# First forward step and last inverse step as single full-precision products, and an earlier first tile table

## The chip, the cores and the metric

The kernel runs on one core of a Trainium2 chip. The metric is the time of one execution on the device in microseconds (us). The engines are TensorE (PE, with its weight loads shown as PEld), VectorE (DVE), ScalarE (ACT), GpSimd (POOL) and SyncE (SP), which issues most DMAs. TensorE's granted clock is shown as a share of 2.4 GHz: 1.00 is 2.4 GHz, 0.50 is 1.2 GHz.

## What is computed

A spectral layer is followed by a mixture of experts. `x` is 8 batches of 2496 tokens with 256 features.

```python
X = np.fft.rfft(x, axis=1)
Yr = Xr @ w_r - Xi @ w_i + b_r          # Yi likewise
Yr = sign(Yr) * maximum(abs(Yr) - 0.01, 0)
y = np.fft.irfft(Yr + 1j * Yi, n=2496, axis=1)
x = y.reshape(19968, 256)
expert = argmax(x @ w_gate, axis=1)     # 8 experts, gate_w is the softmax value
out[rows of e] = gate_w * (maximum(x[rows of e] @ w1[e], 0) @ w2[e])
```

## The kernel before

**Stages.** The transform of length 2496 is done as 39 times 64. `fwd_a` is the first forward step: 11 products `pa` per batch, with 117 (or 78) rows in and 120 out, 512 columns each, written to the scratch `spec` in memory. `turn` reads it back as `t`, `fwd_b` makes the second step (`pb`), `halves` splits the result into a rounded part and a rest (`sh`, `sl`), `mix` multiplies by the weights (`pk`, `pm`), with the sum `kb` of bias and `k` made on GpSimd, and `shrink` applies the threshold (`r`, then four operations `y`). `inv_b` (`pv`, evicted to `z`) and `inv_a` go back: `pz` turns a group of three times 39 tokens upright and computes the gate's logits in the same product, `py` is the last inverse step, evicted by ScalarE to `yb`. A batch has 22 groups. `route` (VectorE work, with one small product `pr` that counts tokens by expert) finds each token's place, and `scatter` sends the rows on GpSimd to a list per expert in memory. The experts then work on tiles of 256 rows.

**Full precision and splits.** PE takes full-precision numbers, or numbers of a rounded type at a higher rate. Most products here use the rounded type three times: rounded part by rounded part, rest by rounded part, rounded part by rest. `split_x` (L269) makes `xh` on ScalarE and `xl` on VectorE from `x`, one step of the schedule ahead of `fwd_a` (L280), which then makes three products `pa` for batches 1 to 7. For batch 0 it makes one full-precision product. In `inv_a` (L387) the bank `pz` is evicted twice, as `zh` by ScalarE and then `zl` by VectorE, and `py` is three products. `pz`, `pb` and `pv` are full-precision products.

**Order.** `spectral` (L411) runs 80 steps (batch b, s from 0 to 9), and PE, SP, ScalarE and VectorE execute in the order in which the code is written. A step begins with `fwd_b` and the first part of `halves` for the next step, `shrink` of the last, then `mix` of its own. The lists `first`, `second`, `loads` and `back` say which `fwd_a`, `split_x`, loads of `x` and `inv_b` fall into it. In the steps with s from 2 to 5 (`turning`) up to three calls of `inv_a` for the batch before are spread over the step by `inverse()`. `tick(n)` advances the oldest waiting `route` or `table` by n pieces (a piece ends at a `yield`), and `send(n)` issues n scatters. Both work through one queue, so more pieces in `route` put its later operations further back in the order.

**Banks and buffers.** `pa`, `pz` and `pv` share four PSUM buffers `u`; `py`, `pk`, `pr` share two, `yo`.

**Tables and the end.** `table(0)` (L638) tells which expert and rows the first five tiles take. It is queued in step s=6 of the last batch and counts all batches but one. `finish_last` (L531) does the last batch's `inv_a`, its `route` and `table(1)`, and runs tiles 0 to 2 between, with `tick` and `send` in them. `experts_rest` runs the others.

Of the kernel before, what the change touches and what calls it, by code (L numbers as in the profile page):

```python
# [10 lines left out]
F32 = mybir.dt.float32  # L11
# [8 lines left out]
S = 2496  # L20
# [78 lines left out]
class Kernel:  # L99
    def __init__(self, tc, nb, x, w_r, w_i, b_r, b_i, w_gate, w1, w2,  # L100
                 c_fa, c_fe, c_ga, c_bm, c_bi, c_ids, c_score, c_base, c_ltri, c_tcol, out):
        self.__dict__.update({n: v for n, v in locals().items() if n != "self"})
        self.nc = tc.nc
        self.ntok = nb * S
        self.cap = TT + self.ntok
        self.nt = (self.ntok + E * (TT - 1)) // TT
        done = (nb - 1) * S
        self.early = EARLY if done - E * (TT - 1) > (EARLY - 1) * TT else 0
        self.spec = [self.nc.dram_tensor(f"spec{i}_dram", (120, G, D), F32, kind="Internal").ap() for i in range(2)]
        self.xs = self.nc.dram_tensor("xs_dram", (E * self.cap, XW), F32, kind="Internal").ap()  # L110
# [31 lines left out]
    def open_inverse(self, st):  # L142
# [24 lines left out]
        self.gar = k.tile([120, 117], F32, name="gar")  # L167
        self.gh = k.tile([120, 117], F32R, name="gh")
        self.gl = k.tile([120, 117], F32R, name="gl")
        self.ids = k.tile([117, nb, G], I32, name="ids")  # L170
# [9 lines left out]
    def open_forward(self, st):  # L180
# [7 lines left out]
        self.far = far = f.tile([117, 120], F32, name="far")  # L188
        self.fh = f.tile([117, 120], F32R, name="fh")
        self.fl = f.tile([117, 120], F32R, name="fl")  # L190
        self.fer = f.tile([78, 120], F32, name="fer")
        self.feh = f.tile([78, 120], F32R, name="feh")
        self.fel = f.tile([78, 120], F32R, name="fel")
        nc.sync.dma_start(far, self.c_fa)
# [41 lines left out]
    def split_constants(self):  # L236
        nc, f, raw = self.nc, self.f, self.raw
        nc.scalar.copy(self.fh, self.far)
        nc.vector.tensor_sub(self.fl, self.far, self.fh)
        nc.scalar.copy(self.feh, self.fer)  # L240
        nc.vector.tensor_sub(self.fel, self.fer, self.feh)
        ws = self.w.tile([128, 2, D], F32, tag="r", name="wsum")
# [4 lines left out]
        for nm in ("s", "d", "r"):  # L247
# [3 lines left out]
            nc.vector.tensor_sub(self.wl[nm], raw[nm], self.wh[nm])  # L251
        nc.scalar.copy(self.gh, self.gar)
        nc.vector.tensor_sub(self.gl, self.gar, self.gh)
        for c in range(2):
# [13 lines left out]

    def split_x(self, b, q, g):  # L269
        nc = self.nc  # L270
        m = 117 if q < 5 else 78
        xt = self.xg[b, q][:m, g:g + 2, :].rearrange("p g d -> p (g d)")
        xh = self.w.tile([117, 512], F32R, tag="xh", name="xh")
        xl = self.w.tile([117, 512], F32R, tag="xl", name="xl")
        nc.scalar.copy(xh[:m, :], xt)  # L275
        nc.vector.tensor_sub(xl[:m, :], xt, xh[:m, :])  # L276
        self.xs2[b, q, g] = xh, xl

    def fwd_a(self, b, q, g):
        nc = self.nc  # L280
        m = 117 if q < 5 else 78
        raw, hi, lo = (self.far, self.fh, self.fl) if q < 5 else (self.fer, self.feh, self.fel)
        p = self.psi.tile([128, 512], F32, tag="u", name="pa", bufs=4)
        if b:
            xh, xl = self.xs2.pop((b, q, g))
            parts = ((hi, xh), (lo, xh), (hi, xl))
        else:
            parts = ((raw, self.xg[b, q][:, g:g + 2, :].rearrange("p g d -> p (g d)")),)
        for i, (a, v) in enumerate(parts):
            nc.tensor.matmul(p[:120, :], a[:m, :], v[:m, :], start=i == 0, stop=i == len(parts) - 1)  # L290
        ae = self.xp.tile([120, 2, D], F32, tag="ae", name="ae", bufs=5)
        to = ae.rearrange("p g d -> p (g d)")
# [94 lines left out]
    def inv_a(self, b, i):  # L387
        nc = self.nc
        for g in (2 * i, 2 * i + 1) if i < GH else ():
            p = self.psi.tile([128, 512], F32, tag="u", name="pz", bufs=4)  # L390
            for c in range(2):
                nc.tensor.matmul(p[:120, c * 136:(c + 1) * 136],
                                 self.z[:, c, 3 * g:3 * g + 3, :].rearrange("p j a -> p (j a)"), self.iw[:, c, :],
                                 start=True, stop=True)
            h = self.wi.tile([120, YW], F32R, tag="zh", name="zh", bufs=4)
            l = self.wi.tile([120, YW], F32R, tag="zl", name="zl", bufs=4)
            nc.scalar.copy(h, p[:120, :YW])
            nc.vector.tensor_sub(l, p[:120, :YW], h)
            self.hl[g] = h, l
        for g in (2 * i - 2, 2 * i - 1) if i else ():  # L400
            if g % GH == 0:
                self.yb = self.wi.tile([117, GH, YW], F32, tag="yb", name="yb", bufs=2)
            h, l = self.hl.pop(g)
            p = self.psi.tile([128, 512], F32, tag="yo", name="py")
            for m, (a, v) in enumerate(((self.gh, h), (self.gl, h), (self.gh, l))):
                nc.tensor.matmul(p[:117, :YW], a, v, start=m == 0, stop=m == 2)
            nc.scalar.copy(self.yb[:, g % GH, :], p[:117, :YW])
            if g % GH == GH - 1:
                self.jobs.append(self.route(b, g // GH, self.yb))

    def spectral(self, fwd):  # L411
        nb = self.nb
        self.t1s, self.pbs, self.ss, self.us, self.ys, self.hl, self.xs2 = {}, {}, {}, {}, {}, {}, {}
        self.jobs, self.rows = [], []
# [21 lines left out]

        first, second, loads, back = ({i: [] for i in range(-1, n)} for _ in range(4))
        for b in range(1, nb):
            at = 10 * b - 10
            for i, o in enumerate((1, 1, 2, 2, 3, 3, 4, 4, 5, 5, 6) if b == 1 else (-3, -2, -1, 0, 0, 1, 2, 3, 4, 5, 6)):  # L440
                first[at + o].append((b, *pairs[i]))
                second[at + o - 1].append((b, *pairs[i]))
            for q, o in enumerate((None, None, 0, 1, 1, 2) if b == 1 else (-7, -5, -4, -2, 0, 2)):
# [10 lines left out]
        for it in range(n):  # L454
            b, s = todo[it]
            late = b == nb - 1
            half, small = iter(()), iter(())
            if it + 1 < n:
                self.fwd_b(*todo[it + 1])
                half = self.halves(*todo[it + 1])  # L460
                next(half)
            if it:
                small = self.shrink(*todo[it - 1])
                next(small)
            next(half, None)
            turning = b and 2 <= s < 6
            turns = iter(range(3 * s - 6, 3 * s - 3) if turning else ())
# [7 lines left out]

            spare = 1 if late else 0
            self.tick(2 + spare)
            inverse()
            mix = self.mix(b, s)
# [6 lines left out]
            next(small, None)  # L486
            for a in second[it]:
                self.split_x(*a)
            self.tick(2 + spare)
# [11 lines left out]
            if it + 4 < n:  # L501
                self.turn(*todo[it + 4])
            if late and self.early and s == 6:
                self.jobs.append(self.table(0))
# [53 lines left out]
    def route(self, b, hf, y):  # L558
# [41 lines left out]
        nc.vector.tensor_copy(sb, pa[:, GH - 1, :])  # L600
        for _ in range(4):
            yield
# [35 lines left out]
    def table(self, last):  # L638
# [70 lines left out]
        if last:  # L709
            lap = rt.tile([128, 128], F32, name="lap")  # L710
            nc.vector.tensor_copy(lap, fin[:, 3:4].broadcast_to((128, 128)))
            yield "pe"
            p = self.psi.tile([128, 512], F32, tag="yo", name="pl")
# [255 lines left out]
```

## Time and profile before

| what | value |
|---|---|
| median of 3 runs | 1668.5 us (1666.49 to 1670.34) |
| the profiled execution's own time | 1668.7 us |
| its span, first to last instruction | 1666.9 us, mean granted clock 0.974 |
| PE busy | 1534.7 us (92%) |
| DVE busy | 1335.3 us (80%) |
| ACT busy | 1116.1 us (67%) |
| POOL busy | 617.5 us (37%) |

Busy time of PE counts overlapping matmuls once, and the ends of matmuls are modelled: the distance between the starts of two of them tells more of their cost than the length of one. A wait in brackets, such as `[3.94 <-DVE sb L600]`, is idle time of the engine ahead of the instruction and what ended it. In the table by stretch the number behind a busy time is a count of instructions.

### The profile page before, as it was taken

What the parts mean: (1) busy time and instruction counts of PE and PEld (TensorE: products, weight loads), DVE (VectorE), ACT (ScalarE), POOL (GpSimd) and SP (SyncE); (2) the same over time, 40 slices, a digit from 0 to 9 for tenths busy, and PEclk for the clock granted to TensorE, in tenths of its full rate; (3) what the DMA queues carried; (4) which work ended last, traced back from release to release, by engine and by line L of the source; (5) the groups of instructions that cost most, each with busy time, mean ns of one, the idle gap of its engine ahead of it and who ended that gap; (6) DMA issues with size and microseconds to landing.
All of it is one profiled execution on the core that took longest, in us unless ns stands there. A gap on an engine that the chain in (4) does not pass through costs nothing. (4 is left out here: it accounts for less than half of the span.)

```text
span 1666.9 us, 36023 instructions
## 1 busy us (share of the span) xinstructions
PE 1534.7 (92%) x10880; PEld 1422.8 (85%) x10880; DVE 1335.3 (80%) x2755; ACT 1116.1 (67%) x2334; POOL 617.5 (37%) x462
## 2 busy tenths in 40 slices
PE   5889898988988887779999999999999999999997
PEld 2778787878878886778999999999999999999996
DVE  2678878888888888668888888888888888888886
ACT  2677777676767665546677677677677667677675
POOL 2121626362535345351333333333333333333332
PEclk8899999999999998999999999999999999999998
DMA  8753535353535311324322312312312313213210
GB/s 249 200 145 94 171 98 161 108 156 107 164 95 148 102 57 46 114 65 102 97 50 46 99 47 46 100 46 60 85 46 61 83 46 96 49 46 91 52 46 19
DMA packets 182932, 153.81 MB, mean 92 GB/s; under 512 B 120378, under 2 KB 154080, under 8 KB 182477
## 3 DMA queue, kind: packets, MB, share of 16 engines
q1 hardware_dynamic: 162829, 107.17, 25.6%
q0 software_dynamic: 19904, 44.29, 8.1%
q8 instruction: 88, 1.44, 0.4%
q14 instruction: 111, 0.91, 0.2%
HBM read 243.33 MB, written 66.37 MB: 186 GB/s over the span
## 5 line engine op out<-in xcount | busy, mean ns | idle before, releaser
L892 POOL DMA_INDIRECT out<-o,row x154 | 303.7, 1972 | 571.2 <-DVE o L890 546.1
L882 PE MATMUL po<-h,hh 128*128 128x512 f32 x1312 | 463.4, 397 | 2.7 <-ACT hh L849 2.7
L844 PE MATMUL ph<-xh,l 128*128 128x256 f32 x1312 | 372.0, 284 | 4.4 <-DVE l L785 4.4
L844 PE MATMUL ph<-xh,h 128*128 128x256 f32 x1312 | 372.4, 284 | 0.6 <-ACT h L784 0.5
L844 PE MATMUL ph<-xl,h 128*128 128x256 f32 x1312 | 371.8, 283 | 0.2 <-DVE xl L827 0.2
L849 ACT ACTIVATE hh<-ph 128x512 fp32r<-128x512 f32 x328 | 196.0, 598 | 251.9 <-PE ph L844 232.5
L850 DVE SCALAR_TENSOR_TENSOR hl<-ph,hh 128x512 fp32r<-128x512 f32 x328 | 226.7, 691 | 150.6 <-ACT hh L849 136.5
L879 PE MATMUL po<-h,hl 128*128 128x256 f32 x1148 | 322.6, 281 | 0.2 <-DVE hl L850 0.2
L882 PEld LDWEIGHTS po<-h,hh 128*128 128x128 f32 x1312 | 242.2, 189 | 47.4 <-ACT hh L849 3.0
L844 PEld LDWEIGHTS ph<-xh,l 128*128 128x128 f32 x1312 | 251.9, 192 | 8.4 <-DVE l L785 4.9
L844 PEld LDWEIGHTS ph<-xh,h 128*128 128x128 f32 x1312 | 251.4, 192 | 1.4 <-ACT h L784 0.7
L844 PEld LDWEIGHTS ph<-xl,h 128*128 128x128 f32 x1312 | 251.9, 192 | 0.4 <-DVE xl L827 0.4
L349 POOL TENSOR_TENSOR kb<-bias,k 128x512 f32<-128x512 f32 x80 | 106.1, 1326 | 332.8 <-ACT k L347 289.8
L879 PEld LDWEIGHTS po<-h,hl 128*128 128x128 f32 x1148 | 217.9, 190 | 4.5 <-DVE hl L850 0.5
L624 POOL DMA_INDIRECT xs_dram<-yb,pos x176 | 182.8, 1039 | 82.4 <-issue 43.6
L785 DVE TENSOR_TENSOR l<-r,h 128x512 fp32r<-128x512 f32 x332 | 206.8, 682 | 3.1 <-ACT h L784 3.0
L800 DVE TENSOR_TENSOR h<-r,h 128x512 fp32r<-128x512 f32 x332 | 206.9, 684 | 2.8 <-ACT h L799 2.8
L784 ACT CAST h<-r 128x512 fp32r<-128x512 f32 x332 | 180.7, 618 | 1.8 <-DMA r<-moe_w 1.8
L799 ACT CAST h<-r 128x512 fp32r<-128x512 f32 x332 | 180.4, 618 | 0.0
L368 DVE SCALAR_TENSOR_TENSOR y<-v,r 64x256 f32<-64x256 f32 x320 | 159.7, 499 | 6.1 <-issue 0.8
L381 PE MATMUL pv<-bi,y 128*128 128x128 f32 x640 | 95.3, 288 | 22.5 <-DVE y L368 20.9
L276 DVE TENSOR_TENSOR xl<-x,xh 117x512 fp32r<-117x512 f32 (+1 forms) x77 | 70.4, 926 | 56.5 <-ACT xh L275 54.7
(190 smaller groups left out, 2927.9 us busy)
## 6 DMA issues: line engine op xcount, KB each, us to landing
r<-moe_w SPq DMA_DIRECT2D x178, 512.0 KB
r<-moe_w SPq DMA_DIRECT2D x632, 128.0 KB
spec_dram<-ae SPq DMA_DIRECT2D x88, 240.0 KB
t<-spec_dram SPq DMA_DIRECT2D x160, 128.0 KB
xq<-xs_dram SPq DMA_DIRECT2D x312, 64.0 KB
x<-x SPq DMA_DIRECT2D x40, 384.0 KB
x<-x SPq DMA_DIRECT2D x40, 84.0 KB
xs_dram<-yb,pos POOLq DMA_INDIRECT x176
```

The costliest lines, as they stand in the source:

```text
L368: nc.vector.scalar_tensor_tensor(out=y[q * 64:q * 64 + 64, kp, :], in0=u[h, q, :], scalar=LAM, in1=r[h, q, :], op0=ALU.add, op1=ALU.min)
L624: i = nc.gpsimd.indirect_dma_start(out=self.xs[:, :], out_offset=bass.IndirectOffsetOnAxis(ap=pos[:n, g:g + 1], axis=0), in_=y[:n, g, 0:XW ...
L784: nc.scalar.copy(hi[:, c, s], v)
L785: nc.vector.tensor_sub(lo[:, c, s], v, hi[:, c, s])
L799: nc.scalar.copy(hi[:, s, :], v)
L800: nc.vector.tensor_sub(lo[:, s, :], v, hi[:, s, :])
L844: nc.tensor.matmul(p[:, i, :], a[:, c, f * 128:(f + 1) * 128], v[:, c, :], start=m == 0, stop=m == 5)
L849: nc.scalar.activation(hh[:, s, :], p, AF.Relu)
L850: nc.vector.scalar_tensor_tensor(out=hl[:, s, :], in0=p, scalar=0.0, in1=hh[:, s, :], op0=ALU.max, op1=ALU.subtract)
L879: nc.tensor.matmul(p[:, :D], hl[:, f - 1, hs], w2[:, f - 1, 0, :], start=False, stop=False)
L882: nc.tensor.matmul(p, hh[:, f, hs], w2[:, f].rearrange("p a d -> p (a d)"), start=f == 0, stop=f == 7)
L892: i = nc.gpsimd.indirect_dma_start(out=self.out[:, :], out_offset=bass.IndirectOffsetOnAxis(ap=at[h], axis=0), in_=o[:, h, :], in_offset=N ...
```

## The change

`fwd_a` now makes one full-precision product for every batch, and `split_x` with its list `second` is gone. `inv_a` evicts `pz` once, in full precision, by ScalarE for even groups and by VectorE for odd ones, and `py` is one full-precision product. The split constants go. `ae` has eight buffers for five. In a turning step the first `inverse()` stands ahead of `shrink` and of the second part of `halves`. `route` has a piece more ahead of `pr` (six more in the last batch). `table(0)` counts all batches but two and is queued in step s=1 of the last batch. `table(1)` asks for its last product four pieces later in place of waiting for the next `tick`.

```diff
-        done = (nb - 1) * S
+        done = (nb - 2) * S
...
-    def split_x(self, b, q, g):
...
-        xh = self.w.tile([117, 512], F32R, tag="xh", name="xh")
-        xl = self.w.tile([117, 512], F32R, tag="xl", name="xl")
-        nc.scalar.copy(xh[:m, :], xt)
-        nc.vector.tensor_sub(xl[:m, :], xt, xh[:m, :])
-        self.xs2[b, q, g] = xh, xl
...
     def fwd_a(self, b, q, g):
         nc = self.nc
         m = 117 if q < 5 else 78
-        raw, hi, lo = (self.far, self.fh, self.fl) if q < 5 else (self.fer, self.feh, self.fel)
         p = self.psi.tile([128, 512], F32, tag="u", name="pa", bufs=4)
-        if b:
-            xh, xl = self.xs2.pop((b, q, g))
-            parts = ((hi, xh), (lo, xh), (hi, xl))
-        else:
-            parts = ((raw, self.xg[b, q][:, g:g + 2, :].rearrange("p g d -> p (g d)")),)
-        for i, (a, v) in enumerate(parts):
-            nc.tensor.matmul(p[:120, :], a[:m, :], v[:m, :], start=i == 0, stop=i == len(parts) - 1)
-        ae = self.xp.tile([120, 2, D], F32, tag="ae", name="ae", bufs=5)
+        nc.tensor.matmul(p[:120, :], (self.far if q < 5 else self.fer)[:m, :],
+                         self.xg[b, q][:m, g:g + 2, :].rearrange("p g d -> p (g d)"), start=True, stop=True)
+        ae = self.xp.tile([120, 2, D], F32, tag="ae", name="ae", bufs=8)
...
-            h = self.wi.tile([120, YW], F32R, tag="zh", name="zh", bufs=4)
-            l = self.wi.tile([120, YW], F32R, tag="zl", name="zl", bufs=4)
-            nc.scalar.copy(h, p[:120, :YW])
-            nc.vector.tensor_sub(l, p[:120, :YW], h)
-            self.hl[g] = h, l
+            h = self.wi.tile([120, YW], F32, tag="zh", name="zh", bufs=4)
+            (nc.vector.tensor_copy if g % 2 else nc.scalar.copy)(h, p[:120, :YW])
+            self.hl[g] = h
...
-            for m, (a, v) in enumerate(((self.gh, h), (self.gl, h), (self.gh, l))):
-                nc.tensor.matmul(p[:117, :YW], a, v, start=m == 0, stop=m == 2)
+            nc.tensor.matmul(p[:117, :YW], self.gar, self.hl.pop(g), start=True, stop=True)
...
             spare = 1 if late else 0
+            if turning:
+                inverse()
+            if it:
+                small = self.shrink(*todo[it - 1])
+                next(small)
+            next(half, None)
             self.tick(2 + spare)
-            inverse()
+            if not turning:
+                inverse()
...
-            for a in second[it]:
-                self.split_x(*a)
...
-            if late and self.early and s == 6:
+            if late and self.early and s == 1:
                 self.jobs.append(self.table(0))
...
-        for _ in range(4):
+        for _ in range(10 if b == self.nb - 1 else 5):
             yield
...
-            yield "pe"
+            for _ in range(4):
+                yield
```

Three places show how instructions moved. The first is VectorE at the border of steps s=7 and s=8 of the fourth batch: `v`, the running sums `scan` of `route`, the three operations of `halves` (`su`, `sl`, `sl`), `sb` and `y`. Before:

```order
L355 TENSOR_TENSOR v<-pm,kb 128x512
L594 TENSOR_TENSOR scan_101<-scan_100 117x88
L594 TENSOR_TENSOR scan_102<-scan_101 117x88
L326 TENSOR_TENSOR su<-re,pb 128x256
L327 TENSOR_TENSOR sl<-pb,sh 128x2x256
L330 TENSOR_TENSOR sl<-su,sh 128x2x128
L594 TENSOR_TENSOR scan_101<-scan_102 117x88
L594 TENSOR_TENSOR scan_102<-scan_101 117x88
L600 CAST sb<-scan_102 117x8
L368 SCALAR_TENSOR_TENSOR y<-v,r 64x256 x2
L276 TENSOR_TENSOR xl<-x,xh 117x512
```

The same place now:

```order
L562 TENSOR_TENSOR scan_99<-scan_98 117x88
L562 TENSOR_TENSOR scan_100<-scan_99 117x88
L327 TENSOR_TENSOR v<-pm,kb 128x512
L562 TENSOR_TENSOR scan_99<-scan_100 117x88
L562 TENSOR_TENSOR scan_100<-scan_99 117x88
L568 CAST sb<-scan_100 117x8
L298 TENSOR_TENSOR su<-re,pb 128x256
L299 TENSOR_TENSOR sl<-pb,sh 128x2x256
L302 TENSOR_TENSOR sl<-su,sh 128x2x128
L340 SCALAR_TENSOR_TENSOR y<-v,r 64x256 x4
```

`sb`, which PE's `pr` reads, moved ahead of `halves`, and `xl` is gone from between the `y`.

The second is ScalarE from the start of the turning step s=3 of the same batch: `re` and `sh` of `halves`, the evictions `zh` of `pz` and `yb` of `py`, `r` of `shrink`. Before:

```order
L324 COPY re<-pb 128x256
L325 CAST sh<-pb 128x2x256
L362 ACTIVATE r<-v,nlam 128x512
L329 CAST sh<-su 128x2x128
L397 CAST zh<-pz 120x272 x2
L407 COPY yb<-py 117x272 x2
L297 COPY ae<-pa 120x512
L347 COPY k<-pk 128x256
L275 CAST xh<-x 117x512
L397 CAST zh<-pz 120x272 x2
```

The same place now:

```order
L296 COPY re<-pb 128x256
L297 CAST sh<-pb 128x2x256
L368 COPY zh<-pz 120x272
L375 COPY yb<-py 117x272 x2
L334 ACTIVATE r<-v,nlam 128x512
L301 CAST sh<-su 128x2x128
L269 COPY ae<-pa 120x512
L319 COPY k<-pk 128x256
L368 COPY zh<-pz 120x272
L375 COPY yb<-py 117x272 x2
```

`zh` and `yb` moved ahead of `r`, one `zh` of each pair went to VectorE, and `xh` is gone.

The third is PE around the product `pn`, with which `table(0)` begins, in the last batch. Before, in step s=7:

```order
L341 MATMUL pk<-whr,sl 128x256
L655 LDWEIGHTS ones_b
L655 MATMUL pn<-carry_b,ones_b 128x8
L381 MATMUL pv<-bi,y 128x128 x4
L341 MATMUL pm<-whd,sh 128x256
```

Now, in step s=2:

```order
L285 MATMUL pb<-bm,t_6706 128x2x64 x4
L364 MATMUL pz<-iw,z 120x136 x4
L623 LDWEIGHTS ones_b
L623 MATMUL pn<-carry_b,ones_b 128x8
L313 MATMUL pk<-whr,sh 128x256
```

`pn` moved five steps ahead, into a step with `pz` and `py`.

## Rows read from the trace of the kernel before

**Rows 1.** Busy time by stretch: the first batch's steps, the six batches after, the last batch's steps, the last inverse, the first three tiles, all other tiles. Columns: the stretch and its length, busy time of PE, PEld, DVE, ACT, POOL (with counts), granted clock, share of DMA, GB/s.
```profile
47.20:105.80 58.60, 48.12 (x342) 44.21 (x341) 42.71 (x84) 41.62 (x89) 10.65 (x9) 0.97 0.64 176
105.80:583.60 477.80, 419.40 (x3180) 395.43 (x3179) 393.18 (x951) 337.38 (x823) 204.00 (x180) 0.97 0.44 127
583.60:672.00 88.40, 71.22 (x525) 66.20 (x523) 70.47 (x190) 48.25 (x117) 46.50 (x43) 0.92 0.17 53
672.00:701.50 29.50, 23.76 (x162) 22.09 (x161) 18.18 (x54) 19.59 (x55) 4.61 (x8) 0.88 0.44 132
701.50:757.00 55.50, 44.92 (x281) 40.31 (x281) 38.11 (x107) 24.74 (x49) 30.09 (x39) 0.91 0.19 61
757.00:1666.90 909.90, 896.87 (x6312) 839.75 (x6309) 761.87 (x1340) 634.51 (x1185) 308.95 (x159) 1.00 0.27 64
```
**Rows 2.** The same table by step, for steps s=7 and s=8 of the fourth batch.
```profile
322.60:328.10 5.50, 5.50 (x47) 5.35 (x46) 5.12 (x18) 2.86 (x8) 2.11 (x3) 1.00 0.68 195
328.10:338.80 10.70, 6.75 (x50) 6.19 (x49) 9.16 (x24) 8.33 (x18) 7.35 (x7) 0.93 0.44 127
```
**Rows 3.** Full-precision products of batch 0 at the start: two weight loads of PEld in order of time (start, duration), and the row by stretch around them.
```profile
9.20 0.18 PEld L290 LDWEIGHTS pa<-x,far 117*120 117x120 f32 x1 [0.24 <-issue]
9.63 0.18 PEld L290 LDWEIGHTS pa<-x,far 117*120 117x120 f32 x1 [0.25 <-issue]
...
8.00:10.00 2.00, 1.29 (x3) 0.65 (x4) 0.00 (x0) 0.17 (x1) 1.27 (x3) 1.00 1.06 234
```
**Rows 4.** PE in order of time in the fourth batch (start, duration, product, count): full-precision `pb` and `pz`, then `py` and `pa` in split form.
```profile
307.27 1.05 PE L313 MATMUL pb<-bm,t 128*128 128x128 f32 x8
308.16 1.09 PE L392 MATMUL pz<-iw,z 128*120 128x136 f32 x8
...
309.21 0.28 PE L406 MATMUL py<-zh,gl 120*117 120x272 f32 x1
...
309.84 0.40 PE L290 MATMUL pa<-xh,fh 117*120 117x512 f32 x1
310.07 0.40 PE L290 MATMUL pa<-xh,fl 117*120 117x512 f32 x1
310.31 0.39 PE L290 MATMUL pa<-xl,fh 117*120 117x512 f32 x1
```
**Rows 5.** Groups of instructions by line and shape in the ten steps of the fourth batch: busy us, mean ns of one, idle before.
```profile
L276 DVE TENSOR_TENSOR xl<-x,xh 117x512 fp32r<-117x512 f32 x10 | 8.8, 888 | 6.9 <-ACT xh L275 6.9
L398 DVE TENSOR_TENSOR zl<-pz,zh 120x272 fp32r<-120x272 f32 x22 | 8.5, 428 | 0.6 <-ACT zh L397 0.6
...
L397 ACT CAST zh<-pz 120x272 fp32r<-120x272 f32 x22 | 7.7, 395 | 2.9 <-PE pz L392 2.8
...
L275 ACT CAST xh<-x 117x512 fp32r<-117x512 f32 x10 | 6.2, 635 | 0.0
```
**Rows 6.** The view of waits, PE alone, over the six batches (105.8 to 583.6): us in total, times, longest.
```profile
PE pr L604 <- DVE sb L600: 23.0, 6, 3.9
PE pk L341 <- ACT yb L407: 10.9, 18, 1.1
PE pv L381 <- DVE y L368: 9.9, 12, 1.6
PE pz L392 <- DVE zl L398: 7.3, 6, 1.2
```
**Rows 7.** Step s=8 of the fourth batch in order of time: VectorE's `sb`, PE's `pr`, and two of the products behind it.
```profile
336.28 0.17 DVE L600 CAST sb<-scan 117x8 bf16<-117x8 f32 x1
...
336.50 0.17 PE L604 MATMUL pr<-sb,ltri 117*117 117x8 bf16 x1 [3.94 <-DVE sb L600]
...
337.49 0.42 PE L341 MATMUL pm<-whs,sh 128*128 128x256 f32 x1
337.70 0.42 PE L341 MATMUL pm<-wls,sh 128*128 128x256 f32 x1
```
**Rows 8.** A step without turning of the first batch in order of time, and the one long line of waits of PE in that batch's steps (47.2 to 105.8).
```profile
94.74 0.89 DVE L276 TENSOR_TENSOR xl<-x,xh 117x512 fp32r<-117x512 f32 x1 [1.10 <-ACT xh L275]
96.55 0.69 DVE L355 TENSOR_TENSOR v<-pm,kb 128x512 f32<-128x512 f32 x1
99.66 1.29 POOL L349 TENSOR_TENSOR kb<-bias,k 128x512 f32<-128x512 f32 x1 [4.58 <-ACT k L347]
100.60 0.90 DVE L276 TENSOR_TENSOR xl<-x,xh 117x512 fp32r<-117x512 f32 x1 [1.09 <-ACT xh L275]
...
PE pv L381 <- DVE y L368: 9.9, 8, 3.5
```
**Rows 9.** Waits of PE in the last batch's steps (583.6 to 672.0), the longest and the third, and the first and the last of 19 operations of a table on VectorE in order of time (from `table(1)`, which has the same operations).
```profile
PE pr L604 <- DVE sb L600: 4.1, 1, 4.1
...
PE pq L706 <- DVE fin L700: 2.9, 1, 2.9
...
715.61 0.16 DVE L667 TENSOR_TENSOR cnt<-cnt,used 128x8 f32<-128x8 f32 x1
...
718.65 0.17 DVE L682 SCALAR_TENSOR_TENSOR ind<-te,ge 128x8 f32<-128x8 f32 x1
```
**Rows 10.** Waits of PE in the last inverse (672.0 to 701.5), and the longest in the first three tiles (701.5 to 757.0).
```profile
PE pr L604 <- DVE sb L600: 2.5, 1, 2.5
...
PE ph L844 <- DVE l L785: 4.0, 1, 4.0
```

More of the change, by code (lines that the diff above doesn't have):

```diff
@@ L167, in open_inverse @@
         self.gar = k.tile([120, 117], F32, name="gar")
-        self.gh = k.tile([120, 117], F32R, name="gh")
-        self.gl = k.tile([120, 117], F32R, name="gl")
         self.ids = k.tile([117, nb, G], I32, name="ids")
@@ L188, in open_forward @@
         self.far = far = f.tile([117, 120], F32, name="far")
-        self.fh = f.tile([117, 120], F32R, name="fh")
-        self.fl = f.tile([117, 120], F32R, name="fl")
         self.fer = f.tile([78, 120], F32, name="fer")
-        self.feh = f.tile([78, 120], F32R, name="feh")
-        self.fel = f.tile([78, 120], F32R, name="fel")
         nc.sync.dma_start(far, self.c_fa)
@@ L237, in split_constants @@
         nc, f, raw = self.nc, self.f, self.raw
[L238 to L241, printed above, removed]
         ws = self.w.tile([128, 2, D], F32, tag="r", name="wsum")
@@ L251, in split_constants @@
             nc.vector.tensor_sub(self.wl[nm], raw[nm], self.wh[nm])
-        nc.scalar.copy(self.gh, self.gar)
-        nc.vector.tensor_sub(self.gl, self.gar, self.gh)
         for c in range(2):
@@ L267, in load_x @@
         self.xg[b, q] = t
-    def split_x(self, b, q, g):
-        nc = self.nc
-        m = 117 if q < 5 else 78
-        xt = self.xg[b, q][:m, g:g + 2, :].rearrange("p g d -> p (g d)")
-        xh = self.w.tile([117, 512], F32R, tag="xh", name="xh")
-        xl = self.w.tile([117, 512], F32R, tag="xl", name="xl")
-        nc.scalar.copy(xh[:m, :], xt)
-        nc.vector.tensor_sub(xl[:m, :], xt, xh[:m, :])
-        self.xs2[b, q, g] = xh, xl
     def fwd_a(self, b, q, g):
@@ L402, in inv_a @@
                 self.yb = self.wi.tile([117, GH, YW], F32, tag="yb", name="yb", bufs=2)
-            h, l = self.hl.pop(g)
             p = self.psi.tile([128, 512], F32, tag="yo", name="py")
-            for m, (a, v) in enumerate(((self.gh, h), (self.gl, h), (self.gh, l))):
-                nc.tensor.matmul(p[:117, :YW], a, v, start=m == 0, stop=m == 2)
+            nc.tensor.matmul(p[:117, :YW], self.gar, self.hl.pop(g), start=True, stop=True)
             nc.scalar.copy(self.yb[:, g % GH, :], p[:117, :YW])
@@ L412, in spectral @@
         nb = self.nb
-        self.t1s, self.pbs, self.ss, self.us, self.ys, self.hl, self.xs2 = {}, {}, {}, {}, {}, {}, {}
+        self.t1s, self.pbs, self.ss, self.us, self.ys, self.hl = {}, {}, {}, {}, {}, {}
         self.jobs, self.rows = [], []
@@ L435, in spectral @@
             pass
-        first, second, loads, back = ({i: [] for i in range(-1, n)} for _ in range(4))
+        first, loads, back = ({i: [] for i in range(n)} for _ in range(3))
         for b in range(1, nb):
@@ L441, in spectral @@
                 first[at + o].append((b, *pairs[i]))
-                second[at + o - 1].append((b, *pairs[i]))
             for q, o in enumerate((None, None, 0, 1, 1, 2) if b == 1 else (-7, -5, -4, -2, 0, 2)):
@@ L457, in spectral @@
             half, small = iter(()), iter(())
+            turning = b and 2 <= s < 6
             if it + 1 < n:
@@ L461, in spectral @@
                 next(half)
[L462 to L466, printed above, removed]
             turns = iter(range(3 * s - 6, 3 * s - 3) if turning else ())
```

## Prediction

> **What bounds the kernel now.** I read the table of stretches first. In the last stretch, 909.9 us of expert tiles, TensorE (PE) is busy almost throughout at a granted clock of 1.00, that is 2.4 GHz [rows 1]; the change touches nothing there, so that time stays. What it touches lies ahead of 757 us: the first batch's steps, six batches alike, the last batch's steps, the last inverse and three early tiles. There PE is busy for 80 to 88% and its mean granted clock is 0.88 to 0.97 [rows 1]. Next I read one batch step by step: in step s=7 (322.6 to 328.1) PE is busy for all of its 5.5 us, and the next step, with the same products, takes 10.7 us [rows 2]. So no engine is simply full: PE loses time at certain places. The view of waits names them for the six batches: `pr` on `sb`, `pk` on the eviction `yb`, `pv` on `y`, `pz` on `zl` [rows 6]. With three smaller lines of the same view (4.4, 1.8 and 1.1) they make 58.4 us, 9.7 per batch. The mean clock of 0.97 over 477.8 us [rows 1] is worth another 14.3 us of full speed, 2.4 per batch: behind the longest wait the `pm` products start 0.21 us apart [rows 7], the pace of the lower level, 1.2 GHz.
>
> **The price of the full-precision products.** One of them shows as two records. With 512 columns these start 0.43 us apart while the granted clock is 1.00 [rows 3], so a product costs 0.86. The split form costs three products that start 0.23 and 0.24 apart, 0.705 [rows 4]. That is +0.155 us for each of 77 products of the forward step: +11.9. For the inverse, with 272 columns, no row exists. Eight full-precision records of 128 columns take 0.89 us, 0.111 each [rows 4]; on the line from there to 0.43 at 512 columns, 272 come at 0.231; in proportion to the columns alone at 0.228. I take 0.46 for two. The split form starts a product every 0.126 us (309.21 to 309.84, five intervals) [rows 4], 0.378 for three. That is +0.083 for each of 176: +14.6. All PE work added is 26.5 us; by place 1.7 in the first batch, 21.2 in the six batches (3.5 each), 1.8 in the last batch, 1.8 in the last inverse.
>
> The Trainium skill weighs in twice on this price. Its "FP8 and Floating Point Precision", section "TensorE Precision Notes", counts four passes for true FP32; its "Perfetto Trace Analysis", section "Engine Utilization", only halves the matmul rate for FP32_LOW_HIGH. By the second a product of 512 columns would cost about one record's 0.43 in all, and the sum would be some 47 us below the work of before instead of 26.5 above; the two records of 0.43 in the trace speak for the first.
>
> **What is taken off the other engines.** Per batch VectorE loses 11 `xl` of 0.888 us and 22 `zl` of 0.428 [rows 5]; it gains 11 plain evictions from the same banks with the same columns, for which I take the same 0.43. That is 9.8 + 9.4 - 4.7 = 14.5 us. ScalarE loses 11 `xh` of 0.635 and half of the 22 `zh` of 0.395 [rows 5]: 11.3 us. PE has the most to do afterwards, so the question is which of its waits stay.
>
> **Which waits go.** (1) `pr` on `sb`, 23.0 us [rows 6]. PE came to `pr` at 332.56 and got `sb` at 336.45 [rows 7]. In VectorE's order `sb` stood behind the three operations of `halves` of the same step. Now it stands ahead of them, with no `xl` before it, while `pr` keeps its place on PE, behind five groups of products. VectorE would have to lag by over 4 us for PE to wait; I take 0, and the half clock behind that wait goes too. (2) `pv` on `y`, 9.9 us in the first batch and as much in the six. In a step without turning the loop runs from `xl` to the next `xl`, 94.74 to 100.60, 5.86 us [rows 8]: `xl`, `y`, `v`, then ScalarE's `r`, `sh`, `z`, `k`, `ae`, `xh`. Without `xh` and `xl` the longest loop is `v`, `r`, `sh`, `z`, `k`, GpSimd's `kb`, `v`: from `v` at 96.55 to the end of `kb` at 100.95 [rows 8], 4.4 us. PE's own work there is that of step s=7, 5.5, less one group of 128 columns, 0.89, plus 0.155: 4.8. So PE sets the step, and I take 0. (3) `pk` on `yb`, `pz` on `zl` and the `py` on `zl` line, 22.6 together. `zh` and `yb` now stand ahead of `r` on ScalarE, and no second operation follows the first eviction, so a bank comes free while PE does `pa` (0.86) or `pk`. I take 0.
>
> **The sum by place**, against the profiled execution's own 1668.7 us (span 1666.9 and 1.8 around it; the median of the runs is 1668.5, so nothing is corrected):
> - Six batches: 79.6 us each, less 9.7 of waits, less 2.4 of clock, plus 3.5 of passes: 71.0, so -8.6 each, -52.
> - First batch, 58.6 us: -9.9 of waits [rows 8], -1.8 for the clock of 0.97, +1.7; 1 us held back for loads of `x`, which PE now waits for itself: -9.
> - Last batch, 88.4 us: its waits sum to 17.2, `pr` 4.1 and `pq` 2.9 the longest [rows 9], and the clock of 0.92 costs 7.1. The table is no cheaper at its new place: from `cnt` to `ind` 19 of its operations take 3.2 us on VectorE [rows 9], so its 36 take 6.1, and they stand in step s=2 ahead of an eviction that a `py` of that step needs. That is near 11 us of VectorE beside 7.9 of PE, so I put a new wait of 4. Some 8 us of waits and half the clock's loss stay: -9.2 - 3.6 + 1.8 = -11.
> - Last inverse, 29.5 us: `pr` on `sb`, 2.5 [rows 10], goes, since `route` asks for `pr` six ticks later; half of the `yb` waits, 1.3, go, and 3 of the 3.5 us that the clock of 0.88 costs; +1.8: -5.
> - Early tiles, 55.5 us: routing and the second table stand half a tile later with the same VectorE work; the 4.0 us wait on `l` [rows 10] gives way to one on `hl`: 0, between -4 and +5.
> - Start: six small splits fewer, beside loads: 0.
>
> The sum is -9 - 52 - 11 - 5 = -77: **1592 us**, 4.6% faster.
>
> **Bounds.** If each wait that goes also takes the refill behind it (some 1.7 us a batch, what 71.0 still exceeds the PE starts by), -62 in the batches, -11, -15, -7, -4: 1570. If a third of the waits and of the half clock stays, -34 in the batches, -6, -5, -2, +5: 1627, taken as 1624.
>
> **The rivals.** *The wait for `sb` stays.* VectorE is busy for 9.16 of the 10.7 us of that step [rows 2]; if that is its own backlog, not waiting for `xh`, `sb` comes late again. Then 23 us of waits and 14 of clock are not regained: 1592 + 37 = 1629. Against it: 14.5 us less work per batch and the margin of 4 us. 0.10.
> *Slower.* The place is the turning steps, where each bank `yo` is handed on by one eviction. If PE waits there and at s=8 for a chain that the splits only ran beside, the waits come back at the next bank, and the passes (0.5 to 0.65 us in such a step) are all that is new: 1668.7 + 26.5 = 1695. It decides from the point where less than 27 of the some 130 us of waits and clock ahead of 757 us come back; `pr` on `sb` with its half clock is more than that alone. 0.04.
> *Cheaper products.* At 0.215 a record PE would have 47 us less to do than before; then ScalarE and the `kb` loop bind, at 62 to 65 us a batch: about 1540. Against it stands 0.43 at the full clock [rows 3]. 0.02.
> *The gain just pays for the passes*, within 0.2%: 0.02.
>
> **Chances.** The forecast, 1570 to 1624, has 0.82, the rivals as above; the range leaves these out. 0.2% is about what a measurement of this kernel can tell from no change. Faster 0.94, same 0.02, slower 0.04.
>
> **What would show it.** Right: batches of 70 to 72 us; `pa` and `py` in pairs of records 0.43 and 0.23 apart; no `pr` on `sb` above 1 us and a granted clock of 1.00 through the six batches; a new wait of some 4 us at a `py` in step s=2 of the last batch. Wrong: `pk` or `pz` waits as long as before, a clock that still falls once per batch, a `pa` that waits for `x`, or the first late tile's loads starting over a tile later than before.

## The result, and the profile after

The changed kernel takes **1612.4 us** (median of 4 runs, 1610.16 to 1612.91), where the kernel before took 1669.4 beside it: a ratio of 0.9657, with an interval from 0.9638 to 0.9675. It is 3.4% faster where 4.6% was forecast, and the range held. The profiled execution took 1612.9 us, span 1611.0.

The table by stretch, cut at the same events of the program as [rows 1], with the same columns:

```profile
46.30:95.00 48.70, 46.97 (x329) 39.90 (x328) 40.81 (x72) 33.55 (x75) 12.11 (x9) 1.00 0.74 214
95.00:537.70 442.70, 423.07 (x2984) 372.88 (x2984) 347.55 (x821) 289.97 (x693) 203.10 (x180) 0.99 0.46 137
537.70:625.80 88.10, 71.76 (x503) 63.68 (x501) 66.12 (x179) 45.10 (x106) 46.47 (x44) 0.95 0.18 54
625.80:652.30 26.50, 23.56 (x140) 20.11 (x139) 13.64 (x38) 17.42 (x44) 2.70 (x4) 0.92 0.48 145
652.30:701.10 48.80, 41.46 (x284) 36.55 (x282) 38.92 (x113) 24.78 (x48) 34.75 (x40) 1.00 0.23 72
701.10:1611.00 909.90, 897.72 (x6311) 840.97 (x6308) 761.60 (x1340) 633.98 (x1184) 306.93 (x159) 0.99 0.26 64
```

Against the forecast by place, in us:

| place | forecast | measured |
|---|---|---|
| start, up to the first batch's steps | 0 | -0.9 |
| first batch | -9 | -9.9 |
| six batches | -52 | -35.1 |
| last batch | -11 | -0.3 |
| last inverse | -5 | -3.0 |
| early tiles | 0 | -6.7 |
| other tiles | 0 | 0 |
| sum | -77 | -55.9 |

So 28 us were missed in the six batches and the last batch, and 7 came in the early tiles, where nothing was expected. The price of the products is not the reason: four records of `py` take 0.92 us (283.19 to 284.11), 0.46 a product, and two of `pa` 0.87 (298.54 to 299.41), as forecast. In order of time on PE:

```profile
283.19 1.08 PE L374 MATMUL py<-zh,gar 120*117 120x272 f32 x4
284.11 1.02 PE L261 MATMUL pa<-x,far 117*120 117x512 f32 x2
...
298.54 1.02 PE L261 MATMUL pa<-x,far 117*120 117x512 f32 x2
299.41 1.05 PE L353 MATMUL pv<-bi,y 128*128 128x128 f32 x8
```

The view of waits of PE over the six batches (95.0 to 537.7) tells what stayed, against [rows 6]:

```profile
PE pr L572 <- DVE scan L562: 5.2, 3, 1.7
PE pr L572 <- issue: 4.8, 2, 3.0
PE py L374 <- ACT k L319: 4.0, 6, 0.7
PE pv L353 <- DVE y L340: 3.0, 6, 0.7
PE pr L572 <- DVE sb L568: 1.4, 1, 1.4
```

With two lines below these (0.3 and 0.2) they make 18.9 us, 3.2 per batch, where 58.4 stood before and none was forecast. `pk` on `yb` and `pz` on `zl` are gone, and `py` on `k` has come. The wait of `pr`, 5.2 + 4.8 + 1.4 = 11.4 us, is half of what it was, though `sb` stands ahead of `halves`; whatever name the view gives, each of these `pr` starts 0.05 us after the end of `sb`. A clock of 0.99 over 442.7 us is some 4 us more. Cut by batch it is 1.00 in four of the six and 0.98 in two, where before the change it fell in each. Steps s=7 and s=8 of the fourth batch in the table by stretch, against [rows 2]:

```profile
296.00:301.70 5.70, 5.70 (x46) 5.21 (x45) 4.41 (x15) 2.67 (x8) 3.00 (x3) 1.00 0.75 225
301.70:309.80 8.10, 6.36 (x48) 5.73 (x47) 7.78 (x22) 5.14 (x13) 4.29 (x4) 0.95 0.38 115
```

The same step s=8 in order of time (VectorE, GpSimd, PE, ScalarE), against [rows 7]:

```profile
300.10 0.42 DVE L298 TENSOR_TENSOR su<-re,pb 128x256 f32<-128x256 f32 x1 [1.09 <-issue]
...
302.10 1.83 DVE L340 SCALAR_TENSOR_TENSOR y<-v,r 64x256 f32<-64x256 f32 x2
...
307.65 0.17 DVE L568 CAST sb<-scan 117x8 bf16<-117x8 f32 x1
...
302.36 1.29 POOL L321 TENSOR_TENSOR kb<-bias,k 128x512 f32<-128x512 f32 x1 [1.62 <-ACT k L319]
...
307.88 0.17 PE L572 MATMUL pr<-sb,ltri 117*117 117x8 bf16 x1 [1.74 <-DVE scan L562]
...
299.04 0.28 ACT L542 ACTIVATE ex<-lg 117x88 f32<-117x88 f32 x1 [3.03 <-DVE mx L539]
299.47 0.59 ACT L297 CAST sh<-pb 128x512 fp32r<-128x512 f32 x1
```

Between `su` and `sb` VectorE has no pause: 7.7 us of work, while PE's step before took 5.7. Two `y` there take 1.83 us instead of 0.85, beside `kb` on GpSimd. Ahead of `su` VectorE paused for 1.09 us, and `su` began as ScalarE's `sh` of `halves` ended (300.06). ScalarE had itself waited 3.03 us for VectorE's `mx`, since `ex`, an exponential of `route`, now stands ahead of that `re` and `sh`; before the change it came 3.9 us after the same `re` (327.66 and 323.72).

In the last batch the time stayed. Its step s=2 in order of time: the first operation of `table(0)` on VectorE, a copy in the middle of it, the `zh` behind it, and PE's `py`:

```profile
552.66 0.16 DVE L625 COPY n<-pn 128x8 f32<-128x8 f32 x1
...
554.81 2.01 DVE L643 COPY ge<-te 128x8 f32<-128x8 f32 x1
...
561.11 0.43 DVE L368 COPY zh<-pz 120x272 f32<-120x272 f32 x1
...
561.68 1.23 PE L374 MATMUL py<-zh,gar 120*117 120x272 f32 x2 [5.20 <-DVE zh L368]
```

The table holds VectorE from 552.66 to 561.11, with two `y` (0.84) among it: 7.6 us, not 6.1, one `ge` of 8 columns alone 2.01. The `zh` behind it is late, and `py` waits 5.2 us (4 were forecast). The longest waits of PE in the last batch's steps; with six more lines of this view they make 16.1 us, where 17.2 stood before:

```profile
PE py L374 <- DVE zh L368: 5.4, 2, 5.2
PE pv L353 <- ACT z L356: 3.1, 1, 3.1
```

### The profile page after: what moved, and what is told of

Its sections match the earlier page's. It is cut to its first block, busy times and chain, and to the rows that moved or that the text cites. A ratio compares the mean times of both kernels' runs of the same rounds, so it can differ in the third digit from the quotient of the medians.

```text
span 1611.0 us, 35135 instructions
## 1 busy us (share of the span) xinstructions
PE 1532.3 (95%) x10627; PEld 1388.9 (86%) x10627; DVE 1279.2 (79%) x2587; ACT 1054.1 (65%) x2166; POOL 618.7 (38%) x460
## 5 line engine op out<-in xcount | busy, mean ns | idle before, releaser
L321 POOL TENSOR_TENSOR kb<-bias,k 128x512 f32<-128x512 f32 x80 | 110.8, 1386 | 296.6 <-ACT k L319 233.2
L340 DVE SCALAR_TENSOR_TENSOR y<-v,r 64x256 f32<-64x256 f32 x320 | 183.0, 572 | 6.0 <-ACT r L334 1.6
L374 PE MATMUL py<-zh,gar 120*117 120x272 f32 x352 | 101.0, 399 | 15.9 <-DVE zh L368 6.6
L375 ACT COPY yb<-py 117x272 f32<-117x272 f32 x176 | 67.2, 389 | 59.0 <-PE py L374 51.9
```

What stands on the lines that cost most here:

```text
L340: nc.vector.scalar_tensor_tensor(out=y[q * 64:q * 64 + 64, kp, :], in0=u[h, q, :], scalar=LAM, in1=r[h, q, :], op0=ALU.add, op1=ALU.min)
```

## The experiments

Theory **W** (work): PE's waits went because the splits left VectorE and ScalarE. Theory **O** (order): they went because `sb`, `zh` and `yb` moved ahead. From the first four runs came the questions of the next eight. The kernel before ran beside each group: 1667 to 1669 us (medians) in the first two, 1661 in the last two, so ratios are compared, not times; where an expectation gives times, they are from a kernel before of 1667 to 1669.

| kernel | us (median) | ratio to before | interval |
|---|---|---|---|
| the changed kernel | 1612.4 | 0.9657 | 0.9638 to 0.9675 |
| passes_only | 1616.3 | 0.9692 | 0.9675 to 0.9708 |
| order_only | 1646.9 | 0.9871 | 0.9855 to 0.9888 |
| fwd_only | 1614.6 | 0.9688 | 0.9672 to 0.9704 |
| inv_only | 1665.2 | 0.9981 | 0.9967 to 0.9994 |
| fwd_end | 1604.3 | 0.9616 | 0.9603 to 0.9629 |
| inv_split | 1605.9 | 0.9631 | 0.9618 to 0.9644 |
| no_turn | 1612.3 | 0.9663 | 0.9650 to 0.9676 |
| tab6 | 1610.0 | 0.9649 | 0.9634 to 0.9664 |
| is_pr7 | 1592.2 | 0.9591 | 0.9571 to 0.9611 |
| end_send | 1607.3 | 0.9685 | 0.9664 to 0.9706 |
| end_pr5 | 1598.0 | 0.9618 | 0.9595 to 0.9641 |
| is_pr7_tab6 | 1584.1 | 0.9533 | 0.9509 to 0.9558 |

### Which part of the change does it

**passes_only** is the changed kernel with the order of before:

```diff
-        ae = self.xp.tile([120, 2, D], F32, tag="ae", name="ae", bufs=8)
+        ae = self.xp.tile([120, 2, D], F32, tag="ae", name="ae", bufs=5)
...
+            if it:
+                small = self.shrink(*todo[it - 1])
+                next(small)
+            next(half, None)
...
-            if turning:
-                inverse()
-            if it:
-                small = self.shrink(*todo[it - 1])
-                next(small)
-            next(half, None)
             self.tick(2 + spare)
-            if not turning:
-                inverse()
+            inverse()
...
-        for _ in range(10 if b == self.nb - 1 else 5):
+        for _ in range(4):
...
-        done = (nb - 2) * S
+        done = (nb - 1) * S
-            if late and self.early and s == 1:
+            if late and self.early and s == 6:
...
-            for _ in range(4):
-                yield
+            yield "pe"
```

> Both full-precision products and no splits, but everything else in the order of the kernel before: shrink ahead of the inverse in turning steps, four pieces of route ahead of pr, table(0) in step s=6 of the last batch from all batches but one, five buffers ae. Theory W (work): the waits went because VectorE and ScalarE have 14.5 and 11.3 us less to do per batch; then most of the gain is here: 1612 to 1630 us, and the wait of pr on sb is under 2 us. Theory O (order): the splits lay beside PE, and the waits went because sb, zh and yb stand further ahead; then this pays the passes, 26.5 us, with the waits of before: 1669 to 1695 us, pr on sb still near 3.9 us per batch.

**order_only** is the other half: the kernel before with these same lines changed the other way.

> The kernel before, splits and three products kept, with only the order of the change: the inverse ahead of shrink in turning steps, five pieces (ten in the last batch) ahead of pr, table(0) in step s=1 of the last batch from all batches but two, four pieces ahead of the last product of table(1), eight buffers ae. Theory W (work): VectorE's backlog stays, so the time is that of before within 10 us: 1659 to 1680. Theory O (order): the waits go without the 26.5 us of passes: 1585 to 1605.

**fwd_only** and **inv_only** each do one product alone in the kernel before:

```diff
-            for a in second[it]:
-                self.split_x(*a)
...
-            parts = ((hi, xh), (lo, xh), (hi, xl))
+        nc.tensor.matmul(p[:120, :], (self.far if q < 5 else self.fer)[:m, :],
+                         self.xg[b, q][:m, g:g + 2, :].rearrange("p g d -> p (g d)"), start=True, stop=True)
```

> The kernel before with only the first forward step as one full-precision product, no xh and xl: VectorE loses 9.8 us and ScalarE 7 per batch, PE gains 11.9 in all. Theory W: the loop through xl (9.9 us of waits of pv in the first batch) goes and pr on sb falls by more than half: 1630 to 1650. Theory O: only the first batch's 9.9 comes back, against 11.9 of passes: 1667 to 1675.

```diff
-            nc.scalar.copy(h, p[:120, :YW])
-            nc.vector.tensor_sub(l, p[:120, :YW], h)
...
+            (nc.vector.tensor_copy if g % 2 else nc.scalar.copy)(h, p[:120, :YW])
...
-            for m, (a, v) in enumerate(((self.gh, h), (self.gl, h), (self.gh, l))):
-                nc.tensor.matmul(p[:117, :YW], a, v, start=m == 0, stop=m == 2)
+            nc.tensor.matmul(p[:117, :YW], self.gar, self.hl.pop(g), start=True, stop=True)
```

> The kernel before with only the last inverse step as one full-precision product and one eviction per bank pz: VectorE loses 4.7 us and ScalarE 4.3 per batch, PE gains 14.6 in all. Theory W: pz on zl (7.3 us) and part of pk on yb go and pr on sb falls by the 1 to 3 us that VectorE is ahead: 1645 to 1665. Theory O: pz on zl goes and nothing else: 1672 to 1680.

Measured: the forward step alone gives 3.1%, as much as both products (passes_only), and the inverse alone 0.2%. Theory W holds for the forward step, by more than it asked (1614.6, not 1630 to 1650), and barely for the inverse (1665.2, its upper end). What it said of `pr` on `sb` was missed: under 2 us in passes_only (12.4 in all, up to 3.4), down by more than half in fwd_only (12.5 of 23.0 stay), down by 1 to 3 us in inv_only (22.4 stay). The order alone gives 1.3%, outside both of its forecasts. The two halves passes_only and order_only, 3.08% and 1.29%, would add to 4.4%, and give 3.4% together: they share a wait. PE's waits in the six batches, of fwd_only, passes_only and order_only:

```profile
PE pr L577 <- DVE sb L573: 10.0, 5, 3.4
PE pk L317 <- ACT yb L383: 9.9, 18, 1.5
PE pr L577 <- DVE scan L567: 2.5, 1, 2.5
```

```profile
PE pr L569 <- DVE sb L565: 12.4, 6, 3.4
PE pk L313 <- ACT yb L375: 3.5, 5, 0.7
```

```profile
PE pv L381 <- DVE y L368: 14.4, 12, 1.6
PE pr L607 <- DVE sb L603: 8.2, 4, 2.1
...
PE pr L607 <- DVE scan L597: 3.0, 1, 3.0
PE pr L607 <- issue: 2.1, 1, 2.1
```

`pr` waits 12.5 us without the splits of `x`, 12.4 without any split, 13.3 with the new order alone, and 11.4 in the changed kernel: from 23.0 each half of the change takes it to 12 or 13, and both together hardly further. Without the inverse's splits `pk` on `yb` falls from 9.9 to 3.5, and the passes take most of that back: a batch takes 72.6 us where it takes 72.8 in fwd_only. By their price the passes are 0.083 x 132 = 11.0 us in these batches; PE's busy time there rises by only 5.9 (413.8 to 419.7), and why it is less is open. In order_only `pv` on `y` grows from 9.9 to 14.4.

### What the changed kernel loses and gains by its parts

**fwd_end** is fwd_only with two pieces of the order:

```diff
-        for _ in range(4):
+        for _ in range(10 if b == self.nb - 1 else 4):
...
-            yield "pe"
+            for _ in range(4):
+                yield
```

> The kernel before with the forward step in full precision and of the new order only two pieces: ten pieces of route ahead of pr in the last batch, and four pieces ahead of the last product of table(1). Inverse split, table(0) in step s=6, turning steps as before. It stands against fwd_only (1614.6). Theory E (the order pays at the end only, through these two): the last inverse loses its pr wait of 2.6 us, the early tiles lose their waits of 4.2, 2.3 and 1.4: 1602 to 1607, below the changed kernel. Theory T (the early tiles gain because table(0) is early): 1611 to 1617.

Theory E is right: 1604.3, 0.7% below fwd_only and 0.4% below the changed kernel. PE's longest waits in the early tiles, up to the same product of tile 3, in fwd_only (55.5 us; two more of 2.6 and 2.1 are gone in fwd_end) and in fwd_end (46.6 us):

```profile
PE ph L817 <- DVE l L758: 4.0, 1, 4.0
```

```profile
PE ph L818 <- DVE hl L824: 2.3, 2, 2.0
PE ph L818 <- ACT h L758: 2.0, 1, 2.0
```

The 6.7 us that the early tiles gave were these two pieces' work; `table(0)` stands in step s=6 here.

**inv_split** is the changed kernel with `zh`, `zl` and three `py` of before; **no_turn** has `shrink` and the rest of `halves` ahead of the inverse again; **tab6** has `table(0)` where it was:

```diff
-            if turning:
-                inverse()
             if it:
                 small = self.shrink(*todo[it - 1])
                 next(small)
             next(half, None)
             self.tick(2 + spare)
-            if not turning:
-                inverse()
+            inverse()
```

```diff
-        done = (nb - 2) * S
+        done = (nb - 1) * S
-            if late and self.early and s == 1:
+            if late and self.early and s == 6:
```

> The changed kernel with the inverse split again: py as three products, zh and zl from each bank. It stands against the changed kernel (1612.4). Theory P (the inverse's passes and its waits cancel, as from fwd_only, 1614.6, to passes_only, 1616.3): 1606 to 1614. Rival (the new order needs the single eviction, since zl stands behind the table and the y): 1618 to 1630.

> The changed kernel with shrink and the second part of halves ahead of the inverse again in turning steps. It stands against the changed kernel (1612.4). Theory D (zh and yb ahead of r only move the wait: pk on yb goes, py on zh and pv on y come): 1606 to 1613, the six batches 72.6 to 73.8 us each. Rival (it is worth the 4.3 us of pk on yb and more): 1616 to 1622.

> The changed kernel with table(0) in step s=6 of the last batch from all batches but one, as before. It stands against the changed kernel (1612.4). Theory S (the 36 small operations of the table stand ahead of a zh, cost a wait of 5.2 us and a half clock of 3.4 in step s=2, and nothing needs them there): 1602 to 1607. Rival (the table only costs elsewhere: pq waits 4.6 again, and the early tiles wait for the first list): 1610 to 1618.

inv_split is 0.26% faster than the changed kernel by ratios whose intervals overlap a little, and 0.3% faster than no_turn, which has the changed kernel's time and ran in its group (1605.9 and 1612.3): with the new order the full-precision inverse costs some 4 to 6 us, and theory P, which let passes and waits cancel, holds at its lower end. no_turn is the same as the changed kernel within the intervals: as theory D had it, `zh` and `yb` ahead of `r` only move waits, though not quite those that it named. PE's waits in the six batches of no_turn:

```profile
PE pv L353 <- DVE y L340: 9.1, 5, 1.8
PE pk L313 <- ACT yb L375: 4.7, 5, 1.3
PE pr L569 <- DVE sb L565: 3.9, 6, 1.6
```

With 0.5 on `pm` they make 18.2 us, where the changed kernel has 18.9: there `pr` waits 11.4 and `pv` 3.0. tab6 comes to 1610.0, not distinguishable from the changed kernel (0.9649 and 0.9657) and not the 1602 to 1607 of theory S. Its last batch is 4 us shorter (84.0); the wait of 5.2 of `py` on `zh` is gone, but two others have come, in kind as the rival said (PE's waits there, 537.0 to 621.0):

```profile
PE pn L623 <- ACT k L319: 2.0, 1, 2.0
PE pq L674 <- DVE fin L668: 1.7, 1, 1.7
```

Of the 4 us, the profiled execution loses 2.4 elsewhere: 1.1 in the six batches (443.8), 0.4 in the last inverse and 0.9 in the tiles.

### Why pr still waits

**is_pr7** is inv_split with seven pieces of `route` ahead of `pr` in place of five:

```diff
-        for _ in range(10 if b == self.nb - 1 else 5):
+        for _ in range(10 if b == self.nb - 1 else 7):
```

> inv_split (1605.9) with seven pieces of route ahead of pr in place of five, in all batches but the last, so PE comes to pr two pieces later. In inv_split pr still waits 12.6 us for VectorE in the six batches. Theory P (only the place of pr is wrong): these waits go, 1593 to 1597. Theory B (backlog: VectorE is some 2 us behind PE by step s=8 whatever stands there): pr waits no more, but pv on y or pk waits as long, 1603 to 1609.

**end_pr5** has 5 in place of 4 in the same line of fwd_end:

> fwd_end (1604.3) with five pieces of route ahead of pr in place of four in all batches but the last, as in the change, with nothing else of its order. Theory P (place): the 13.4 us of pr on sb fall by a piece of the step, 1 us or more per batch: 1594 to 1598. Theory B (backlog): the wait moves to pv or pk: 1601 to 1607.

**end_send** spreads the scatters of fwd_end otherwise:

```diff
-            self.send(4 if late else 3)
+            self.send(4 if late or s < 2 else 6 if s < 4 else 4 if s < 7 else 1)
```

> fwd_end (1604.3) with the same scatters spread otherwise in all batches but the last: four per step in s=0, 1, 4, 5 and 6, six in s=2 and 3, one in s=7, 8 and 9, in place of three in each. Theory G (a pair of y takes 1.9 us in place of 0.85 while scatters run on GpSimd, and this sets VectorE's backlog at s=8): the pairs there fall to 0.85 to 1.2, pr waits under 6 us in the six batches where it is 13.4 now, 1592 to 1599. Rival (the backlog is route's and halves' own work, or the slow pairs come back in the turning steps and hold evictions): 1601 to 1612.

end_pr5 has the ratio of fwd_end (0.9618 and 0.9616), and is_pr7 is 0.40% below inv_split. PE's waits in the six batches: end_pr5, then inv_split, then is_pr7.

```profile
PE pv L357 <- DVE y L344: 9.0, 5, 1.8
PE pr L577 <- DVE sb L573: 4.0, 6, 1.6
```

```profile
PE pr L580 <- DVE scan L570: 9.9, 5, 3.0
...
PE pv L357 <- DVE y L344: 2.1, 3, 0.7
PE pr L580 <- DVE sb L576: 1.7, 1, 1.7
```

```profile
PE pv L357 <- DVE y L344: 6.3, 7, 1.6
```

One piece later, `pr` loses 8.5 us of its 12.5 and `pv` gains 9.0, at the same ratio: theory B, a backlog of VectorE that only changes the name of the wait. (Its 1598.0 us lie in theory P's range only because the kernel before was 8 us faster beside it.) Two pieces later than inv_split, `pr` loses its 11.6 and `pv` gains 4.2, and 0.40% of the time is gained, between the two theories. But the edit moves more than `pr`. In all six batches of the changed kernel, of order_only and of inv_split VectorE pauses 1.09 us ahead of the `su` in step s=7, with `ex` ahead of `re` on ScalarE; in is_pr7, as in end_pr5 and no_turn, `ex` stands behind `re` and that pause is gone. Whether is_pr7 gains by the place of `pr` or by this is not shown; no_turn, without the pause, gains nothing. (The profiled executions of end_pr5 and end_send took 1592.2 and 1600.8, the least of all executions of these two, and `pk` on `yb` is 3.3 us in both where fwd_end has 9.7; what sets that is open, so their rows are read for `pr` and `pv` alone.)

end_send is slower (0.9685), against theory G, and `pr` there waits longer. With one scatter a step pairs of `y` are as slow, and the slow ones stand beside `kb` (VectorE and GpSimd in order of time):

```profile
299.62 2.34 DVE L344 SCALAR_TENSOR_TENSOR y<-v,r 64x256 f32<-64x256 f32 x2
...
299.92 1.31 POOL L325 TENSOR_TENSOR kb<-bias,k 128x512 f32<-128x512 f32 x1
...
```

Sorted by what runs beside them, 231 of the 320 `y` of that run overlap no `kb` and take 0.42 us on average, at most 0.50, with a scatter beside them or not; the 89 that overlap a `kb` take 1.10 on average and up to 2.15. Theory G named the wrong work of GpSimd, and the rival's time holds.

**is_pr7_tab6** puts the two edits together that is_pr7 and tab6 make.

> is_pr7 (ratio to the kernel before 0.9591) with table(0) in step s=6 of the last batch from all batches but one. Theory A (the terms add: the table's place costs the last batch 2 to 4 us, whatever stands around it, as from the changed kernel, 0.9657, to tab6, 0.9649): ratio 0.9565 to 0.9585, the last batch's steps 86 to 89 us where they are 92.3, and the wait of py on zl of 5.5 us there gone. Rival (the table's work is only moved, and pn and pq wait for it in place of py): ratio 0.9585 to 0.9605.

It has the ratio 0.9533, below both forecasts, and is the fastest of all: 1.3% below the changed kernel. The stretch of its last batch and of its last inverse:

```profile
515.90:601.40 85.50, 69.72 (x524) 64.48 (x523) 72.82 (x198) 49.53 (x121) 47.69 (x44) 0.94 0.19 57
601.40:625.60 24.20, 20.36 (x162) 19.43 (x162) 17.77 (x50) 19.77 (x55) 2.17 (x4) 1.00 0.51 156
```

The last batch lost 6.0 us (91.5 in is_pr7, cut at the same events) and the last inverse 1.9. That the table's move is worth more here than in tab6 was not forecast and was not taken further.

## Why the prediction was right, and where it was not

- **Direction and mechanism** hold: the passes cost no more than was forecast (0.46 and 0.87 a product where records follow each other), and the waits that the splits caused on VectorE and ScalarE were worth more. But of the two products only the forward step's gave a gain. For the inverse the sum of 14.6 us of passes against the waits on `yb` and `zl` comes to about zero with the old order and to a loss with the new one; the prediction gave the waits to the change as a whole and didn't set them against each product's own price.
- **The step that failed** is the one on `pr`: "VectorE would have to lag by over 4 us for PE to wait; I take 0". VectorE lagged by more: `sb` ended 6.1 us after PE had begun the step (307.82 against 301.70), and PE asked for it after 4.4 (306.14). VectorE had worked 7.7 us without a pause from `su` to `sb`, 1.0 us of it the two slow `y`, and `su` had come late by the pause of 1.09 that the new place of `ex` made. 11.4 of the 23.0 us stayed. The rival "the wait for `sb` stays" was half right, and mostly for the reason that it gives, VectorE's own backlog. Three signs that the prediction set for itself were not met: no `pr` on `sb` above 1 us, a clock of 1.00 through the six batches, and batches of 70 to 72 us (73.8).
- **The relief of VectorE** was smaller than put. Its busy time in the six batches fell from 393.2 to 347.6 us, 7.6 a batch, where the prediction took off 14.5. Busy time counts overlapping operations once, which makes part of the difference; the rest is mostly operations that became longer, as the last section shows.
- **Other waits taken as 0**: `py` on `k` 4.0, which is new, and `pv` on `y`, of which 3.0 of 9.9 us stayed in the six batches. With `pr`, the small ones, and some 4 us at half clock, the six batches kept 23 us that the sum had struck out; they fell by 35.1, not 52. By these terms a batch is 79.6 - 6.6 of waits - 1.7 of clock + 3.5 = 74.8 us, and 73.8 were measured. The last 1.0 is about what the passes fell short of their price: PE's busy time rose by 3.7 us in the six batches, by some 14 if the 10 us that the better clock took off are added back, where 21.2 were put.
- **Last batch**: mis-sized. The table's wait was foreseen (4 us; 5.2 came), but the waits of the last batch were to fall from 17.2 to 8 us in all, and they sum to 16.1. The clock's part nearly came: from 0.92 to 0.95 it is 2.7 us of the 3.6 forecast.
- **Last inverse**: -5 forecast, -3.0 measured. `pr` no longer waits there, but the clock of 0.92 still costs some 2 us, where 0.5 was left, and `py` waits 1.2 for a `zh` of VectorE.
- **Early tiles**: forecast 0, measured -6.7. Its bound of -4 was too near; fwd_end shows that the later pieces of `route` and `table(1)` do this. That they helped the total was luck, but the range did not need it: without them the time would be 1619.
- **First batch**: -9 forecast, -9.9 measured. The wait of `pv` on `y` is gone [rows 8], and the clock stays at 1.00.

## What to carry to other kernels

Price each part of a change against the waits that this part alone causes: here one product's splits carried the gain, and the other's could have stayed. A wait on an engine that runs behind doesn't go by moving the operation that it names; count that engine's work from the last point where it stood idle to that operation, with the durations that it has at that place, look at what held it idle there, and at what asks next.

## What the runs showed of the hardware

Operations on VectorE that overlap `kb`, a `tensor_tensor` on GpSimd of some 1.3 us, can be held until it has ended: of the 89 `y` that overlap one in end_send, 50 take 1.40 us or more, and every one of these ends 0.28 to 0.30 us after its `kb`, also where it began up to 0.56 before it; the other 39 take 0.42 at most. Two `y` above took 1.83 us instead of 0.85, and the copy of 8 columns in the table 2.01, to 0.03 after its `kb`. Scatters on GpSimd had no such effect on `y` (0.42 either way), and the 18 `zh` on VectorE, copies from PSUM, that overlap a `kb` in the six batches of the changed kernel kept their 0.44. So VectorE's work of a step depends on where it stands; the groups by line of the six batches, before and after the change, show it (busy time, mean ns):

```profile
L276 DVE TENSOR_TENSOR xl<-x,xh 117x512 fp32r<-117x512 f32 (+1 forms) x63 | 60.5, 968 | 42.0 <-ACT xh L275 40.3 <-ACT ae L297 1.3
L368 DVE SCALAR_TENSOR_TENSOR y<-v,r 64x256 f32<-64x256 f32 x240 | 119.1, 496 | 3.4
```

```profile
L340 DVE SCALAR_TENSOR_TENSOR y<-v,r 64x256 f32<-64x256 f32 x239 | 134.9, 565 | 3.3
```

The same `y` take 15.8 us more, which the sum, made from the durations of before, did not have; in the same views the running sums `scan` rise from 11.8 to 18.1 and `lg` from 3.9 to 8.9. Before the change `xl` bore part of this: one takes 0.69 us alone (338.26) and 0.97 on average here, 35 of the 63 beside a `kb`. With `xl` gone, 85 `y` overlap a `kb` where 42 did.

The Trainium skill's "SBUF — State Buffer", section "Who interferes with whom", says that VectorE and GpSimd share a pair of ports, that an operation of VectorE with two inputs from SBUF contends for it with a GpSimd operation that reads SBUF, and one in a mode that uses both pairs with GpSimd in any case, and that the one that issues first holds the pair for its whole instruction while the other blocks. The durations of `y`, which has two such inputs, and of `zh`, which reads PSUM alone, agree with it; that `kb` is the cause was not tried by taking it off GpSimd.
